# Strassen's seven block products for the second matrix product of an attention and MLP kernel on one core

## The chip, the cores and the metric

One Trainium2 chip, of which the kernel uses one core. The metric is the device time of one execution, in microseconds. Of the kernel before there are three timed runs, with a median of 689.35 us (686.24 to 691.3), and one profiled execution with a span of 687.8 us.

## What is computed

For each of 8 batches there are 8 heads of 512 tokens of 64 numbers, and 32 state rows per head. Tokens read the state and the state reads the tokens, both by softmax attention. The 544 rows of a batch (512 tokens, 32 state rows), with the heads side by side as 512 numbers, then pass through a normalized two-layer MLP with a residual.

```python
scores = scale * np.matmul(x, state.transpose(0, 1, 3, 2))
a = np.exp(scores - scores.max(-1, keepdims=True)); a /= a.sum(-1, keepdims=True) + 1e-09
xread = np.matmul(a, state)
scores2 = scale * np.matmul(state, x.transpose(0, 1, 3, 2))
a2 = ...                                   # the same softmax
sread = np.matmul(a2, x)
x = np.concatenate([xread, sread], axis=2) # then B, S, H*D: 8 x 544 x 512
xn = (x - mu) / np.sqrt(var + 1e-06) * g_ln
out = x + np.maximum(xn @ w_ch1, 0.0) @ w_ch2   # 512 x 2048, 2048 x 512
```

## The kernel before

**Precision.** A number of a large product is held as the sum of two float16 numbers, a high half and a low half. A product is three matmuls, high times high, high times low and low times high (`TERMS`), which add up in PSUM. A high half is made by a ScalarE copy, a low half by an instruction that subtracts the high half from the value.

**Tiles.** The 2048 hidden numbers are 4 units `u` of 512, each of 4 blocks of 128. The 512 tokens of a batch are 4 blocks `c` of 128. `ea` holds the softmax weights of the tokens over the state rows, by two groups `g` of 4 heads.

**Stages of a batch.** `attention` (L225 and on) loads x and state, makes the scores (L320, into a pair of banks called `banks`), transposes them on VectorE (`ts`), subtracts the maximum on GpSimd, takes the exponential on ScalarE, multiplies with the reciprocal sum on GpSimd, and transposes back (`ef`, then `ea`). `ea` is sent by DMA into `ek`, from which L432 makes the residual rows `xr`; bn_stats, `mv`, `rs` and `rf` are its moments. `eb` is the other softmax, for the state rows. `state_products` (L577) multiplies the state with the first weights, into `matrix`: per unit and head group one product L582, one ScalarE copy and one VectorE instruction. The first layer of a batch is then `matrix` times `ea`: `first_products` (L605), L616, 6 matmuls of 512 columns for each of 16 blocks. `hidden` (L595) takes each bank through ScalarE (relu into `strip`, copy to the high half) and VectorE (low half); for batch 0 GpSimd makes the low half. The four units stay in `hid`. `second_products` (L691) has 48 matmuls of 512 columns (L683) per token block in one PSUM bank, one VectorE instruction that scales and adds to `xr`, and a store per two blocks. Batch 0 goes by units (L706), since its weights arrive late. The 256 state rows of all batches come last: `state_hidden` (L648) with L668, matmuls of 256 columns, and the same second product.

**PSUM.** 5 banks `acc`, one pair `banks`, one bank `spread`.

**Order.** Each stage is a stream of instructions. Three strings, `PLAN` (start to batch 1), `BATCH` (2 to 5) and `LAST`, say which piece of which stream is issued next (`issue`, L190). Each engine then works through its own instructions in that order, waiting for those of other engines where they are needed. Nearly all of them pass through one helper and stand at L110 in the profile, and at L166 in the changed kernel.

Of the kernel before, what the change touches and what calls it, by code (L numbers as in the profile page):

```python
# [14 lines left out]
ALU = mybir.AluOpType  # L15
# [12 lines left out]
SW = 2.0**13  # L28
CM = 2.0**-14
SH = 2.0**-12  # L30
SB = 2.0**14
# [74 lines left out]
def do(f, *args, **kw):  # L106

    def now(v):
        return v() if isinstance(v, Later) else v
    return lambda: f(*map(now, args), **{k: now(v) for k, v in kw.items()})  # L110


@with_exitstack
def moe_attention(ctx: ExitStack, tc: tile.TileContext, x, state, g_ln, w1, w2, out):

# [664 lines left out]
```

## Time and profile before

| what | value |
|---|---|
| three runs, median | 689.35 us |
| lowest, highest | 686.24, 691.3 us |
| span of the profiled execution | 687.8 us |
| median less that span | 1.55 us |
| DMA traffic | 69.36 MB, mean 101 GB/s |
| HBM read, written | 28.05 MB, 9.44 MB |

An entry of the page with an engine shows busy time, its share of the span and the count of its instructions. The rows of digits cut the span in 40 equal slices, each digit the busy share in tenths; `PEclk` is the clock that TensorE was granted, 9 for the full one. Rows of groups have line, engine, operation, output and inputs, shapes and count, then busy time and the mean in nanoseconds of one, then the idle time ahead of them and who ended it. A row of the chain has start, length and what ran. A row of the timeline has in brackets how long the engine was idle ahead of it. PE is TensorE, PEld its weight loads, DVE is VectorE, ACT ScalarE, POOL GpSimd. Matmuls overlap, so the spacing of many in a row tells their cost, not the mean of one.

### The profile page before, as it was taken

Reading aid. Unit: us, or ns where it says so; the run is one execution under the profiler, and the core shown is the slowest. Engines: PE = TensorE matmul, PEld = TensorE weight load, DVE = VectorE, ACT = ScalarE, POOL = GpSimd, SP = SyncE. Lnnn points to the kernel's source line nnn. Section 1 sums busy time; section 2 is a strip of 40 time slices with the busy share of each in tenths; the row PEclk is TensorE's granted clock in tenths of the full one; section 3 lists DMA queues with packets and bytes.
Section 4 is the critical chain, followed back from the end, with each engine's and each line's share of the span. In section 5 each row is a group of like instructions: output and inputs, shape, how many; then the busy total and the mean of one; then the engine's idle time right before and its main releaser. Section 6 shows DMA issues by size and latency. Waiting matters only on the chain.

```text
span 687.8 us, 10177 instructions
## 1 busy us (share of the span) xinstructions
PE 646.6 (94%) x4068; PEld 314.3 (46%) x4068; DVE 373.7 (54%) x668; ACT 362.4 (53%) x588; POOL 67.5 (10%) x54
## 2 busy tenths in 40 slices
PE   1667899999999999999999999999999999999997
PEld 0224655544444444444444444444444444447653
DVE  5988999656634447264536544654366834521020
ACT  5387888796422754186327631774168615712120
POOL 0000463400200002000200020001100110100000
PEclk9866999999999999999999999999999999999999
DMA  8989984826061041504151415121590330120011
GB/s 322 286 263 222 245 206 116 164 45 137 31 165 63 1 81 36 159 34 81 31 155 42 81 31 130 66 52 32 141 213 16 68 83 32 61 47 1 1 61 31
DMA packets 98544, 69.36 MB, mean 101 GB/s; under 512 B 72704, under 2 KB 90624, under 8 KB 98048
## 3 DMA queue, kind: packets, MB, share of 16 engines
q1 hardware_dynamic: 96384, 64.77, 36.6%
q0 software_dynamic: 864, 3.15, 2.5%
q10 hardware_dynamic: 1248, 0.79, 0.4%
q8 instruction: 32, 0.52, 0.3%
q14 instruction: 16, 0.13, 0.1%
HBM read 28.05 MB, written 9.44 MB: 55 GB/s over the span
## 4 chain that ended last, share of the span: by engine, by line
PE 84%; DVE 7%; DMA 3%; ACT 3%; issue 1%; SPq 1%; ACTq 0%; DVEq 0%
PE acc L683 48%; PE acc L616 22%; PE acc L582 4%; PE acc L668 3%; PE acc L516 3%; DVE w_t L110 2%; PE banks L396 1%; PE banks L432 1%; PE banks L320 1%; DVE matrix L110 1%; ACT raw L110 1%; PE banks L409 1%; DMA x_f<-in_x_dram 1%; DMA ek<-ek 1%; DVE x L110 1%
## 5 line engine op out<-in xcount | busy, mean ns | idle before, releaser
L683 PE MATMUL acc<-w2h,hid 128*128 128x512 f16 x1632 | 363.4, 379 | 0.0
L683 PEld LDWEIGHTS <-hid 128*128 128x128 f16 x1632 | 157.1, 98 | 192.5 <-issue 9.3
L616 PE MATMUL acc<-ea,matrix 128*128 128x512 f16 (+1 forms) x864 | 175.2, 356 | 0.9 <-DVE matrix L110 0.7
L616 PEld LDWEIGHTS <-matrix 128*128 128x128 f16 x864 | 82.6, 98 | 82.8 <-ACT matrix L110 2.9
L110 DVE TENSOR_TENSOR hid<-strip,hid 128x512 f16<-128x512 f32 x120 | 81.0, 685 | 66.3 <-ACT hid L110 65.7
L110 ACT ACTIVATE strip<-acc,hs 128x512 f32<-128x512 f32 x112 | 75.5, 681 | 53.6 <-PE acc L616 40.4
L110 ACT ACTIVATE hid<-strip 128x512 f16<-128x512 f32 x136 | 82.9, 625 | 15.7 <-PE acc L683 13.6
L110 ACT ACTIVATE matrix<-acc 128x512 f16<-128x512 f32 x64 | 35.7, 599 | 91.6 <-PE acc L582 91.6
L110 DVE SCALAR_TENSOR_TENSOR xr<-acc,of_second,xr 128x512 f32<-128x512 f32 x28 | 20.9, 747 | 88.5 <-PE acc L683 88.4
L110 DVE SCALAR_TENSOR_TENSOR matrix<-acc,matrix 128x512 f16<-128x512 f32 x64 | 42.1, 679 | 11.6 <-ACT matrix L110 11.5
L110 POOL TENSOR_TENSOR ts<-ts,mA 128x1024 f32<-128x1024 f32 (+1 forms) x8 | 14.4, 1802 | 230.6 <-DVE mA L110 230.6
L582 PE MATMUL acc<-w1c,sT 128*32 128x512 f16 x512 | 36.2, 389 | 0.3 <-DMA w1c<-raw 0.3
L110 DVE BATCH_NORM_STATS2 s<-xr 128x6 f32<-128x512 f32 x32 | 21.6, 679 | 16.4 <-ACT xr L110 16.4
L110 POOL TENSOR_TENSOR rs<-rs,mhalf 128x4 f32<-128x4 f32 (+1 forms) x10 | 10.3, 1031 | 192.3 <-DVE rs L110 192.3
L110 POOL TENSOR_TENSOR hid<-strip,hid 128x512 f16<-128x512 f32 x16 | 22.9, 1486 | 45.4 <-ACT hid L110 44.7
L516 PE MATMUL acc<-w_t,gm 128*128 128x512 f32 x32 | 21.0, 823 | 6.3 <-DVE w_t L110 6.3
L110 DVE SCALAR_TENSOR_TENSOR x<-x_f,x_s,x 128x512 f16<-128x512 f32 x32 | 25.7, 833 | 1.9 <-ACT x L110 1.8
L110 ACT ACTIVATE xr<-banks,ux 128x1024 f32<-128x1024 f32 x14 | 15.5, 1109 | 19.7 <-PE banks L432 19.7
L110 ACT ACTIVATE x<-x_f,x_s 128x512 f16<-128x512 f32 x32 | 21.4, 713 | 7.9 <-DVE x_s L110 7.9
L110 ACT ACTIVATE strip<-acc,hr 128x512 f32<-128x512 f32 x8 | 5.4, 684 | 35.6 <-PE acc L668 34.9
L110 DVE TENSOR_REDUCE mB<-banks 128x2 f32<-128x1024 f32 x7 | 8.5, 1217 | 27.9 <-PE banks L320 27.9
L110 ACT ACTIVATE ea<-ef 128x1024 f16<-128x1024 f32 (+1 forms) x9 | 8.6, 960 | 26.6 <-DVE ef L110 26.6
(114 smaller groups left out, 524.1 us busy)
## 6 DMA issues: line engine op xcount, KB each, us to landing
raw<-in_moe_w_ch_dram SPq DMA_DIRECT2D x16, 1024.0 KB, 7.8
out_dram<-xr SPq DMA_DIRECT2D x16, 512.0 KB, 2.7
x_f<-in_x_dram SPq DMA_DIRECT2D x15, 512.0 KB, 5.8
w1c<-raw SPq DMA_DIRECT2D x16, 256.0 KB, 6.2
ek<-ea SPq DMA_DIRECT2D x56, 64.0 KB, 2.0
ek<-ek SPq DMA_DIRECT2D x7, 512.0 KB, 7.7
xr<-part POOLq DMA_DIRECT2D x6, 512.0 KB, 5.9
high<-w1c SPq DMA_DIRECT2D x8, 256.0 KB, 7.2
```

Source lines behind the costliest of these rows:

```text
L110: return lambda: f(*map(now, args), **{k: now(v) for k, v in kw.items()})
L320: nc.tensor.matmul(o[32 * j:32 * j + 32], lhsT=sT[:, g, a, 32 * j:32 * j + 32], rhs=xT[:, s, 4 * g + j].rearrange("p c t -> p (c t)"), sta ...
L396: nc.tensor.matmul(ps_z[:, h // 4, :, h % 4], lhsT=xv[:, c // hc, h, c % hc], rhs=ebT[:, :, h // 4, c, 32 * (h % 4):32 * (h % 4) + 32], st ...
L409: nc.tensor.matmul(pr[:, g], lhsT=z4[:, g, i], rhs=fold, start=i == 0, stop=i == 1, skip_group_check=True)
L432: nc.tensor.matmul(px[:, c, D * h:D * h + D], lhsT=ek[:, h // 4, h % 4, (2 * t + c) * P:(2 * t + c + 1) * P], rhs=sk[:, h], start=True, st ...
L516: nc.tensor.matmul(ps, lhsT=gm[:, k:k + 1].broadcast_to([P, P]), rhs=t4[:, k], start=k == 0, stop=k == 3)
L582: nc.tensor.matmul(ps[32 * j:32 * j + 32], lhsT=sT[:, g, a, 32 * j:32 * j + 32], rhs=w[:, 2 * g + j // 2, j % 2], start=a == 0, stop=a == ...
L616: nc.tensor.matmul(o, lhsT=m[:, g, i, P * q:P * q + P], rhs=ea[:, s, k, g], start=g == 0 and n == 0 and (b > 0 or q % 2 == 0), stop=g == 1 ...
L668: nc.tensor.matmul(ps[:, 256 * f:256 * f + 256].rearrange("p (t n) -> p t n", t=2), lhsT=w[:, k // 2, k % 2, fs] if k < H else wn[:, k - H ...
L683: nc.tensor.matmul(po, lhsT=hid[:, i, q, c * P:(c + 1) * P], rhs=w[:, j, q], start=first and q == 0 and n == 0, stop=last and q == 3 and n ...
```

## The change

For batches 1 to 7 and the state rows the second product is made by Strassen's method: both factors are cut in 2 by 2 blocks, seven products of sums of blocks take the place of eight, and the result is put together by additions. A piece of work is now 256 tokens (a group `g`) and a unit of 512 hidden numbers: 256 × 512 times 512 × 512, in blocks of 128 tokens × 256 and 256 × 256.

- **First product.** `first` (L770) makes 24 matmuls of 256 columns per piece, into a pair of banks named `pair` with one buffer. `state_products` of batches 1 to 7 uses the same pair and reads both halves with one ScalarE and one VectorE instruction of 1024 numbers, where there were two of 512 each. The state rows have `first_of_state` (L779).
- **Sums of the left factor.** One ScalarE relu of 1024 numbers fills `rs`. VectorE makes three sums of 256, GpSimd one. The seven operands `xs`: ScalarE copies the high halves (768 for the three plain blocks, 1024 for the four sums), VectorE makes the low half of the 768 and GpSimd of the 1024. `rs` and `xs` have two buffers each, by turns of the pieces.
- **The seven products.** `strassen_products` (L808): 42 matmuls of 256 columns per piece, in four parts, into four `acc` banks that a group holds over its four units.
- **Putting together.** Per group one ScalarE copy of 512, four VectorE additions from PSUM (256, 512, 256, 512), one GpSimd addition of 256, then two VectorE instructions add to `xr`, and a store.
- **Sums of the right factor.** `sums_of_weights`, once per unit: per half, GpSimd adds the halves (1024) and makes four sums of 256, ScalarE and VectorE make the float16 halves of these, one of which replaces a block of the weights.
- **PSUM** is now 4 banks `acc`, the pair `banks` and the pair `pair`; what used `spread` takes a bank of the others.
- **Scales** `SH`, `SB` and the bound of the second weights change by a factor of two.
- **Order.** One string `PLAN` with entries "stream:index" orders the whole program, written anew for all of it.

The core of the diff:

```diff
+S2 = 2.0**12
-SH = 2.0**-12
-SB = 2.0**14
+SH = 2.0**-13
+SB = 2.0**15
...
 PLAN = (
-    "b3 b0 d0 b1 b4 b2 b5-6 a0 b7-11 b22 b12 b72 b24 b13 b19 b17 d3 b23 d2 b25 b14 b20 b18 d1 d5-6 d4 d7 e1 "
...
+    "1:1 1:3 1:0 1:2 1:4-7 0:0 1:8-12 2:1 2:6 2:0 1:17-18 2:5 2:7 2:3 1:13 1:22-23 2:2 4:1 4:5 1:24 2:4 4:6 1:25 4:7 "
...
-    ps_f = ctx.enter_context(tc.tile_pool(name="ps_f", bufs=5, space=PSUM))
+    ps_f = ctx.enter_context(tc.tile_pool(name="ps_f", bufs=4, space=PSUM))
     ps_a = ctx.enter_context(tc.tile_pool(name="ps_a", bufs=1, space=PSUM))
-    ps_x = ctx.enter_context(tc.tile_pool(name="ps_x", bufs=1, space=PSUM))
+    ps_d = ctx.enter_context(tc.tile_pool(name="ps_d", bufs=1, space=PSUM))
...
+    sums = main.tile([P, 3 * 2048], F32, name="sums")
+    strip = main.tile([P, 3 * 512], F32, name="strip")
...
             for g in range(G):
-                ps = accumulator()
-                yield do(multiply, ps, g, sT, w1c[u])
-                yield do(nc.scalar.activation, m[:, g, 0], ps, AF.Copy, scale=CM)
-                yield do(nc.vector.scalar_tensor_tensor, m[:, g, 1], ps, CM, m[:, g, 0], ALU.mult, ALU.subtract)
+                if b == 0 or g == 0:
+                    two = accumulator() if b == 0 else pair()
+                yield do(multiply, two if b == 0 else two[:, g], g, sT, w1c[u])
+                if b == 0 or g == 1:
+                    ps, v = (two, m[:, g]) if b == 0 else (two, m.rearrange("p g i f -> p i g f"))
+                    v = [v[:, i] for i in range(2)]
+                    yield do(nc.scalar.activation, v[0], ps, AF.Copy, scale=CM)
+                    yield do(nc.vector.scalar_tensor_tensor, v[1], ps, CM, v[0], ALU.mult, ALU.subtract)
...
+    def sums_of_weights(u):
+
+        w = w2h[u].rearrange("p i (k n) e -> p i n k e", n=2)
+        t = unit(u, "w2_sums").rearrange("p (i k e) -> p i k e", i=2, k=2)
+        s = t[:, 1].rearrange("p k (x e) -> p (k x) e", x=2)
+        (b21, b22), (b11, b12) = ([t[:, 0, k, 256 * x:256 * x + 256] for x in range(2)] for k in range(2))
+        for n in range(2):
+            yield do(nc.gpsimd.tensor_tensor, t[:, 0], w[:, 0, n], w[:, 1, n], ALU.add)
+            yield do(nc.gpsimd.tensor_tensor, s[:, 0], b12, b11, ALU.subtract)
+            yield do(nc.gpsimd.tensor_tensor, s[:, 2], s[:, 0], b22, ALU.subtract)
+            yield do(nc.gpsimd.tensor_tensor, s[:, 3], b21, s[:, 2], ALU.add)
+            yield do(nc.gpsimd.tensor_tensor, s[:, 1], b22, b12, ALU.subtract)
+            v = [w[:, i, n, 1, 256:512] for i in range(2)]
+            yield do(nc.scalar.activation, v[0], s[:, 0], AF.Copy)
+            yield do(nc.vector.tensor_tensor, v[1], s[:, 0], v[0], ALU.subtract)
+            v = [sums16[:, u, :, i, n] for i in range(2)]
+            yield do(nc.scalar.activation, v[0], s[:, 1:4], AF.Copy)
+            yield do(nc.vector.tensor_tensor, v[1], s[:, 1:4], v[0], ALU.subtract)
...
+                def strassen_hidden(b=b, g=g, u=u, ps=ps, x=x, r=r, s=s):
+                    if b < B:
+                        yield do(first, ps, g, u, matrix[b][u], ea)
...
+                    yield do(nc.scalar.activation, r.rearrange("p n (k t) e -> p k n (t e)", k=2),
+                             ps.rearrange("p k (n e) -> p k n e", n=2), AF.Relu, scale=(hs if b < B else hr)[:, u:u + 1])
+                    a12, a22, a11, a21 = (r[:, :, k] for k in range(4))
+                    d = r[:, :, 0:3].rearrange("p n k t -> p k n t")
+                    yield do(nc.vector.tensor_tensor, s[:, 0], a11, a21, ALU.subtract)
+                    yield do(nc.gpsimd.tensor_tensor, s[:, 2], a21, a22, ALU.add)
+                    yield do(nc.scalar.activation, x[:, 0:3, :, 0], d, AF.Copy)
+                    yield do(nc.vector.tensor_tensor, s[:, 1], s[:, 0], a22, ALU.subtract)
+                    yield do(nc.vector.tensor_tensor, s[:, 3], a12, s[:, 1], ALU.add)
+                    yield do(nc.vector.tensor_tensor, x[:, 0:3, :, 1], d, x[:, 0:3, :, 0], ALU.subtract)
+                    yield do(nc.scalar.activation, x[:, 3:7, :, 0], s, AF.Copy)
+                    yield do(nc.gpsimd.tensor_tensor, x[:, 3:7, :, 1], s, x[:, 3:7, :, 0], ALU.subtract)
...
+                                nc.tensor.matmul(po[o], lhsT=x[:, o, n, i], rhs=v[j],
+                                                 start=u == 0 and n == 0 and k == 0 and o in (2, 1, 4, 3),
+                                                 stop=u == U - 1 and n == 1 and k == 2, skip_group_check=True)
+                    for ops in ((2, 0, 1), (4,), (3, 5), (6,)):
+                        yield do(lambda po, *a, ops=ops: multiply(ops, [v() for v in po], *a), po, x, w2h[u], sums16[:, u])
...
+                yield do(nc.scalar.activation, c[:, 0:2], two[0], AF.Copy)
+                yield do(nc.vector.tensor_tensor, c[:, 4], bank[1][:, 0:256], c[:, 1], ALU.add)
+                yield do(nc.gpsimd.tensor_tensor, c[:, 1], c[:, 1], c[:, 0], ALU.add)
+                yield do(nc.vector.tensor_tensor, c[:, 2:4], two[2], c[:, 4:5].broadcast_to([P, 2, 256]), ALU.add)
+                yield do(nc.vector.tensor_tensor, c[:, 4], bank[2][:, 0:256], c[:, 3], ALU.add)
+                yield do(nc.vector.tensor_tensor, c[:, 2:4], two[3], c[:, 2:4], ALU.add)
```

Two places show what the new order does. First VectorE in the softmax of one of the middle batches, before:

```order
L110 TENSOR_REDUCE mB_2557<-banks_2540 128x2
L110 SCALAR_TENSOR_TENSOR sk_93<-s_r_2324,x_s_2390,sk_93 64x512
L110 TENSOR_SCALAR mB_2557<-mB_2557,es_2523 128x2
L110 STREAM_TRANSPOSE ts_2588<-banks_2540 128x1024
L110 TENSOR_REDUCE mA_2590<-ts_2588 128x32
L110 SCALAR_TENSOR_TENSOR eb_2597<-eB_2594,eb_2597 128x1024
L110 TENSOR_REDUCE dA_2632<-ts_2588 128x32
L110 TENSOR_TENSOR hid_2525<-strip_2528,hid_2525 128x512
```

The same engine in the group whose first bank is acc_3973, with the change; the `strip` rows put together the group before it (acc_3577 to acc_3580), and matrix_4119 is what the second state product waits for:

```order
L166 TENSOR_TENSOR strip_71<-acc_3578,strip_71 128x512
L166 TENSOR_TENSOR rs_3889<-rs_3889 128x256 x3
L166 SCALAR_TENSOR_TENSOR sk_95<-s_r_3335,x_s_3654,sk_95 64x512
L166 TENSOR_REDUCE dA_4002<-ts_3909 128x32
L166 TENSOR_TENSOR rs_4004<-rs_4004 128x256 x3
L166 TENSOR_TENSOR xs_4010<-rs_3889,xs_4010 128x6x128
...
L166 SCALAR_TENSOR_TENSOR eb_4042<-eB_4028,eb_4042 128x1024
L166 TENSOR_SCALAR rB_4039<-rB_4039,x_i_3652 128x2
L166 TENSOR_TENSOR rs_4071<-rs_4071 128x256
L166 SCALAR_TENSOR_TENSOR matrix_4119<-pair_4096,matrix_4119 128x2x512
```

Where one `hid` row stood between the softmax's rows, the rows of two pieces stand now, and a matrix row behind them all.

Second, GpSimd in the middle batches. Before, a whole batch, from the softmax of one (ts_2588) to that of the next (ts_3278):

```order
L110 TENSOR_TENSOR ts_2588<-ts_2588,mA_2590 128x1024
L110 TENSOR_TENSOR ts_2588<-ts_2588,dA_2632 128x1024
L110 TENSOR_TENSOR rs_2944<-rs_2944,mhalf_84 128x4
L110 TENSOR_TENSOR ts_3278<-ts_3278,mA_3280 128x1024
L110 TENSOR_TENSOR ts_3278<-ts_3278,dA_3322 128x1024
```

With the change, in the softmax of one batch (ts_4869):

```order
L166 TENSOR_TENSOR xs_4953<-rs_4833,xs_4953 128x8x128
L166 TENSOR_TENSOR rs_4838<-rs_4838,mhalf_86 128x4
L166 TENSOR_TENSOR ts_4869<-ts_4869,mA_4901 128x1024
L166 TENSOR_TENSOR rs_4899<-rs_4899 128x256
L166 TENSOR_TENSOR ts_4869<-ts_4869,dA_5066 128x1024
L166 TENSOR_TENSOR xs_5111<-rs_4899,xs_5111 128x8x128
L166 TENSOR_TENSOR rs_4980<-rs_4980 128x256
L166 TENSOR_TENSOR xs_5195<-rs_4980,xs_5195 128x8x128
```

Between and around the two rows of the softmax now stand the additions (rs, 256 numbers) and the low halves (xs, 1024) of the pieces, a pair of rows for each piece of work.

More of the change, by code (lines that the diff above doesn't have):

```diff
@@ L110, in do, with issue @@
     return lambda: f(*map(now, args), **{k: now(v) for k, v in kw.items()})
+def issue(tc, streams, plan):
+    streams = [list(s) for s in streams]
+    with tc.manual_schedule():
+        for item in plan.split() or [f"{k}:0-{len(s)}" for k, s in enumerate(streams)]:
+            k, n = item.split(":")
+            n = [int(v) for v in n.split("-")]
+            for f in streams[int(k)][n[0]:n[-1] + 1]:
+                f()
 @with_exitstack
@@ L172, in odd @@
         return block(8, "residual_1", 1, name)
-    def spare(name):
-        return block(8, "convert", 1, name)
     def accumulator():
@@ new lines, in multiply @@
+                for f in range(2):
+                    for g in range(G):
+                        for n, (i, k) in enumerate(TERMS):
+                            nc.tensor.matmul(o[:, 256 * f:256 * f + 256], lhsT=m[:, g, i, P * (q + f):P * (q + f) + P],
+                                             rhs=ea[:, s, k, g], start=f == 0 and g == 0 and n == 0,
+                                             stop=g == 1 and n == 2, skip_group_check=True)
+            for s in range(2):
+                for q in (0, 2):
+                    ps = accumulator()
+                    yield do(multiply, ps, s, q, matrix[0][u], ea)
+                    yield from hidden(ps, SH, *(h[:, i, q:q + 2, 256 * s:256 * s + 256] for i in range(2)), 2, nc.gpsimd)
@@ new lines, in moe_attention, with high_halves, state_rows @@
+    high, state_rows_T = [None] * U, [None]
+    def high_halves(u):
+        high[u] = quad("high").bitcast(F16).rearrange("p (k f) -> p k f", k=4)
+        for s in range(2):
+            half = slice(64 * s, 64 * s + 64)
+            yield do(nc.sync.dma_start, out=high[u][half], in_=w1c[u][half, :, s])
+    def state_rows():
+        xs = [r[:, 0:1] for r in residual(B, "xs")[1]]
+        results.append(((None, xs),))
+        for t in range(2):
+            yield do(nc.sync.dma_start, out=xs[t][:, 0], in_=sread_rows[P * t:P * t + P, :])
+        xsT = rows("xsT").bitcast(F16)[:, 0:24 * P].rearrange("p (t k n) -> p t k n", t=2, k=12)
+        state_rows_T[0] = xsT
+        mv, rs = yield from moments([xs[t][:, 0] for t in range(2)])
+        xn = rows("xn")
+        for t in range(2):
+            xt = xn[:, DM * t:DM * t + DM]
+            yield do(nc.vector.tensor_scalar, xt, xs[t][:, 0], mv[:, t, 0:1], rs[:, t:t + 1], ALU.subtract, ALU.mult)
+            v = xt.rearrange("p (h d) -> p h d", h=H)
+            pc = halves("pc")[:, 0:12 * P]
+            hi = pc[:, 0:8 * P].rearrange("p (h i d) -> p h i d", h=H, i=2)
+            lo = pc[:, 8 * P:12 * P].rearrange("p (h d) -> p h d", h=H)
+            yield do(nc.scalar.activation, hi, v.unsqueeze(2).broadcast_to([P, H, 2, D]), AF.Copy, scale=SN)
+            yield do(nc.vector.scalar_tensor_tensor, lo, v, SN, hi[:, :, 0], ALU.mult, ALU.subtract)
+            yield do(nc.sync.dma_start_transpose, out=xsT[:, t], in_=pc)
```

246 lines of the change are left out of this document (116 added, 130 removed), and 143 rows, old and new, of tables (BATCH, LAST, PLAN).

## The prediction, made before the changed kernel was run

> **What bounds the kernel now.** First the page: how full each engine is, when, and what the chain that ended last is made of.
>
> ```profile
> span 687.8 us, 10177 instructions
> PE 646.6 (94%) x4068; PEld 314.3 (46%) x4068; DVE 373.7 (54%) x668; ACT 362.4 (53%) x588; POOL 67.5 (10%) x54
> PE   1667899999999999999999999999999999999997
> PEclk9866999999999999999999999999999999999999
> PE 84%; DVE 7%; DMA 3%; ACT 3%; issue 1%; SPq 1%; ACTq 0%; DVEq 0%
> PE acc L683 48%; PE acc L616 22%; PE acc L582 4%; PE acc L668 3%; PE acc L516 3%; DVE w_t L110 2%; PE banks L396 1%; PE banks L432 1%; PE banks L320 1%; DVE matrix L110 1%; ACT raw L110 1%; PE banks L409 1%; DMA x_f<-in_x_dram 1%; DMA ek<-ek 1%; DVE x L110 1%
> ```
>
> TensorE is full from about the sixth slice on, at a full granted clock. The second product (L683) alone is 48% of the chain, the first (L616) 22%. Next the chain in order of time, where rows of back-to-back matmuls give the price of one, and then the steady stretch.
>
> ```profile
> 295.11 1.40 PE acc L616 x6
> ...
> 366.22 1.40 PE acc L616 x6
> ...
> 600.55 20.72 PE acc L683 x96
> ...
> 626.48 5.24 PE acc L668 x48
> ```
>
> ```profile
> 100.00:120.00 20.00, 20.00 (x151) 10.51 (x149) 19.07 (x35) 17.88 (x25) 7.57 (x7) 1.00 0.46 120
> 240.00:320.00 80.00, 80.00 (x486) 36.59 (x484) 42.95 (x78) 43.51 (x76) 4.83 (x3) 1.00 0.31 73
> 320.00:400.00 80.00, 80.00 (x491) 36.53 (x493) 39.44 (x72) 40.37 (x71) 4.84 (x3) 1.00 0.33 77
> 400.00:480.00 80.00, 80.00 (x498) 36.53 (x487) 43.37 (x74) 42.53 (x74) 6.74 (x4) 1.00 0.27 66
> ```
>
> A matmul of 512 columns takes 20.72/96 = 215.8 ns, one of 256 columns 5.24/48 = 109.2 ns. A batch takes 71.1 us (366.22 − 295.11). In the windows the columns after the length are PE, PEld, DVE, ACT and POOL: PE has no gap in 240 us, DVE is busy 41.9 of 80, ACT 42.1, POOL 5.5. So the bound is the number of matmul columns. Only PE counts, as long as the others keep up.
>
> **What PE saves.** 1440 of the 1632 matmuls of L683 go (192 stay for batch 0), 2520 of 256 columns come: 1440 × 215.8 = 310.8 us become 2520 × 109.2 = 275.2, −35.6. The first products of batches 1 to 7, 672 of 512 columns, become 1344 of 256: 145.0 to 146.8, +1.8. The rows of these forms:
>
> ```profile
> L683 PE MATMUL acc<-w2h,hid 128*128 128x512 f16 x1632 | 363.4, 379 | 0.0
> L683 PEld LDWEIGHTS <-hid 128*128 128x128 f16 x1632 | 157.1, 98 | 192.5 <-issue 9.3
> L616 PE MATMUL acc<-ea,matrix 128*128 128x512 f16 x672 | 153.2, 379 | 0.9 <-DVE matrix L110 0.7 <-ACT matrix L110 0.2
> ```
>
> (379 ns is one pipelined matmul's latency; the spacing is 215.8.) A weight load takes 98 ns and each narrow matmul needs its own. The L668 row is such a stream, a load per matmul, and still runs at 109.2, so I take the load as hidden. **Sum for PE: −33.8 us**; a batch would take 71.1 − 4.9 = 66.2 us, a step of one unit and 256 tokens a little over 8.2.
>
> **What the other engines get.** The prices:
>
> ```profile
> L110 DVE TENSOR_TENSOR hid<-strip,hid 128x512 f16<-128x512 f32 x120 | 81.0, 685 | 66.3 <-ACT hid L110 65.7
> L110 DVE TENSOR_TENSOR ts<-ts,dA 128x512 f32<-128x512 f32 x1 | 0.7, 691 | 0.0
> L221 DVE TENSOR_TENSOR fold<-idf 128x64 f32<-128x64 f32 x1 | 0.2, 224 | 0.3 <-POOL idf masks.py:199 0.3
> L110 DVE SCALAR_TENSOR_TENSOR matrix<-acc,matrix 128x512 f16<-128x512 f32 x64 | 42.1, 679 | 11.6 <-ACT matrix L110 11.5
> L110 POOL TENSOR_TENSOR ts<-ts,dA 128x1024 f32<-128x1024 f32 x7 | 13.4, 1911 | 23.4 <-DVE dA L110 22.0 <-DVE of_weights L110 1.4
> L110 POOL TENSOR_TENSOR ts<-ts,dA 128x512 f32<-128x512 f32 x1 | 1.0, 1047 | 2.5 <-DVE mB L110 2.5
> L110 POOL TENSOR_TENSOR hid<-strip,hid 128x512 f16<-128x512 f32 x16 | 22.9, 1486 | 45.4 <-ACT hid L110 44.7 <-DVE raw L110 0.6
> L110 ACT ACTIVATE xr<-banks,ux 128x1024 f32<-128x1024 f32 x14 | 15.5, 1109 | 19.7 <-PE banks L432 19.7
> ```
>
> DVE's 224 ns for 64 elements and 691 for 512 put a 256 one at 0.42, a 768 one at 0.96, a 1024 one at 1.2. POOL's 1047 and 1911 put a 256 one at 0.62; its 1024 low half lies between 1.91 and 2.97 (twice 1486), and I take 2.1. Per step DVE now has three rs adds and the low half of three operands, 2.2 us; POOL one add and the low half of four operands, 2.7; ACT relu and two copies, near 3.0. Per batch DVE gains 8 × 2.2, four matrix low halves at 1.2 and twice the 2.2 of `together`, and loses 16 × 0.685 and 8 × 0.679: 37.3 (41.9 × 71.1/80) becomes about 48 of 66 us. ACT goes from 37.5 to 41, POOL from 4.9 to 28. None alone is full. The question is whether DVE and POOL can be busy at the same time.
>
> ```profile
> 77.95 3.49 POOL L110 TENSOR_TENSOR hid<-strip,hid 128x512 f16<-128x512 f32 x2 [39.74 <-ACT hid L110]
> ```
>
> ```profile
> 78.76 1.66 DVE L110 SCALAR_TENSOR_TENSOR x<-x_f,x_s,x 128x512 f16<-128x512 f32 x1
> ...
> 158.63 0.75 DVE L110 SCALAR_TENSOR_TENSOR x<-x_f,x_s,x 128x512 f16<-128x512 f32 x1
> ...
> 335.88 1.51 DVE L110 SCALAR_TENSOR_TENSOR eb<-eB,eb 128x1024 f16<-128x1024 f32 x1 [1.61 <-ACT eb L110]
> 337.52 1.22 DVE L110 TENSOR_REDUCE dA<-ts 128x32 f32<-128x1024 f32 x1
> ```
>
> The same DVE instruction took 1.66 us where a POOL add ran and 0.75 where none did. Its two tensors lie in SBUF. So do those of most new DVE work: rs and xs 17.8 per batch, the residual 3.0, eb, ea, sk and x about 6.5. With POOL's 28 that is 55 of 66 us if the two exclude each other: enough room on average, little within a step. A DVE tensor_tensor beside POOL is not in the trace; its delay lies between nothing and the rest of the POOL instruction, and I take it as the scalar_tensor_tensor row shows, the nearest kind.
>
> The Trainium skill, "SBUF — State Buffer", section "Who interferes with whom", states that a DVE instruction with two SBUF inputs contends with a GpSimd instruction that reads SBUF, as an exclusive lock for the whole instruction, whoever starts first. The 1.66 against 0.75 agrees; tensor_tensor no row here shows. By the page the delay comes whenever the two meet, which is the second rival below; with no lock it would be the first.
>
> **The heavy groups: +21 us.** Of the 15 groups of 256 tokens, six also carry the next batch's softmax. I walked the one whose second state product goes to pair_4153. That product needs matrix_4119 (the low half on DVE has to have read pair_4096, the pair's only buffer). From the group's first Strassen product PE has 96 narrow matmuls to it (10.5) and one state product (L582: 4% of 687.8 over 512 matmuls, 54 ns each, 16 of them 0.9): 11.4 us. On DVE stand ahead of it, in its order: four adds of `together` (2.2), six rs adds (2.5), sk (0.75), dA (1.2), the xs low half (0.96), eb (1.5), one more rs (0.42) and some ten small ones (2.0): 11.5, and 1.2 of its own, 12.7. That is 1.3 late with no blocking, if each starts when the one before it ends. POOL has 8.3 in the same stretch (two low halves 4.2, the ts multiply 1.9, two adds 1.2, a power 1.0); what does not hide behind DVE's reads of PSUM, its reduction and its small work, up to some 4.5 and waits of a microsecond, comes on top, so 7 at most. What waits is PE's queue: behind that state product stand the rest of the Strassen products. A second heavy group, walked the same way, came to 5. The ends are 0 and 7 per group (in the first, other work of PE hides the 1.3); the walks come to 7 and 5 with blocking and to about 1 without, so the middle, 3.5 × 6 = **21** (0 to 42). Light groups have 8 us a step against DVE's and POOL's 5 together: **+1** (0 to 3).
>
> **The change-over to batch 1: +8 us.** Here the softmax of batch 1 is a chain that PE has to cover:
>
> ```profile
> 176.91 1.17 DVE ts L110
> ...
> 190.87 1.23 DVE ea L110
> ...
> 203.74 0.77 PE banks L432 x16
> ```
>
> From the transposed scores to ea it took 15.2 us, from there to the matmuls on ek 11.6, all under the second product of other units. In the new order PE has after the scores four second products (48 × 215.8 = 10.4) and a state product (0.4) before the first L770, which needs ea: up to 4.3 short. Then 24 matmuls (2.6) and a state product (0.9) before L491, which needs ek: up to 8.0 more. Both together 0 to 12.3; the second gap stands right behind the first and PE's order leaves it nothing else, so I take two thirds, 8. The block sums cost POOL 8 × (1.9 + 4 × 0.62) = 35 us and DVE 11 in that stretch, ahead of the first low halves on POOL's queue; in the window 100 to 120 DVE has 1 us free of 20, POOL 12. Without cover there the first xs would be late, part of the upper end.
>
> **The end: +1.5.** One residual add after the last matmul (of the 0.75 kind) becomes the rest of `together` (an add of 0.69 and the first residual add), and the last low half on POOL has one step to hide in: 1 to 3.
>
> **Sum**, against the profiled 687.8: −33.8 + 21 + 1 + 8 + 1.5 = −2.3, 685.5. The median of the runs is 1.55 above the span, so **687.0**: no change that can be told. 1% is 6.9 us, about what a measurement of this kernel can tell from no change (682.5 to 696.2). The forecast's own range is 680 to 697, which is 2.3 to 5.2 us per heavy group.
>
> **Rivals.** *The cover holds.* ACT and DVE wait little for POOL, the matrices come at most 1.5 late, PE's saving stays: heavy groups 1 each, change-over 5, end and light 3: −33.8 + 14 = −19.8, 669.5 (657 to 682). For it: the steady rows leave DVE half the time free before, x and rs have two buffers, a step of slack. Against it: the pair has one buffer, and the walk is late even without blocking.
>
> *DVE and POOL take turns and become the bound*, in the heavy groups: a low half on DVE stands behind a POOL low half of 2.1 us again and again, 6.5 per group, 39 in all, change-over 10, end and light 4: −33.8 + 53 = +19, 708 (697 to 716), slower. It decides from 5 us per heavy group. For it: the 1.66 us row, and that POOL's share grows sixfold. Against it: transposes, reductions and PSUM reads on DVE are not delayed in the rows beside POOL, and 55 of 66 us leaves 11.
>
> *Narrow matmuls do not run at 109 ns*: were each 5 ns dearer (only 11 ns lie between it and the load's 98), 3864 of them cost 19 us, 707 on the forecast's sum. The L668 row speaks against it.
>
> **Chances.** Forecast 0.37, cover holds 0.36, taking turns 0.22, dear matmuls 0.05. Faster by over 1%: nearly all of the second and a sliver of the first, 0.41; within 1%: 0.28; slower: 0.31. The range goes from 662 (change-over and heavy groups both near nothing) to 713 (all near their upper ends).
>
> **What would show it.** Right: PE's L808 rows at 109 ns back to back; PE idle of 20 to 30 us in six places between 200 and 600 us, released by DVE matrix or xs; a gap of several us before L770 and L491 near 180; DVE rs and xs rows longer than 0.42 and 0.96 where POOL runs. Wrong: PE without gaps in 240 to 480 and a batch in 66 us (the first rival); a period over 72 (the second); L808 rows over 112 ns apart.

## The result, and the profile after

The changed kernel took 741.19 us (median of 4 runs, 740.43 to 744.35) against 690.25 for the kernel before in the same comparison: a ratio of 1.0766, with a 95% interval of 1.0727 to 1.0805. It is 51 us slower; the forecast of 687 and its range to 713 are both missed. The profiled execution has a span of 742.5 us against 687.8 before, 54.7 more. The ratios here and below are of undisturbed executions; a few took far longer, among them the profiled one of e12 (2235 us), whose rows are not used.

The page of the changed kernel, the lines that answer to those shown of before:

```profile
span 742.5 us, 14084 instructions
PE 635.7 (86%) x5818; PEld 491.5 (66%) x5820; DVE 573.0 (77%) x836; ACT 403.0 (54%) x531; POOL 319.4 (43%) x229
PE   2567988674998969988997999898989998999996
PEclk9878989878999989999999999999999999999999
PE 29%; DVE 27%; issue 6%; ACT 5%; DMA 3%; POOL 3%; SPq 3%; DVEq 0%; ACTq 0%; POOLq 0%
```

TensorE is no longer what the chain consists of: 84% became 29%, and VectorE stands beside it with 27%. PE is busy 10.9 us less (635.7 for 646.6), where the count of columns promised 33.8 less, and idle 106.8 us where it was 41.2. So the 54.7 us are −33.8 of work, +22.9 in which the same work ran more slowly, and +65.6 of waiting. Added up by who ended them, PE's waits for VectorE grew from 24.0 to 55.0 us, those for DMA from 3.7 to 21.4 and those for ScalarE from 9.3 to 21.1; GpSimd itself ended 2.4 us of them.

The groups by form, with the count, busy time and mean of one as before:

```profile
L166 POOL TENSOR_TENSOR xs<-rs,xs 128x1024 f16<-128x1024 f32 x60 | 134.1, 2235 | 153.9 <-ACT xs L166 150.1
L166 DVE TENSOR_TENSOR rs<-rs 128x256 f32<-128x256 f32 x180 | 115.4, 645 | 50.0 <-ACT rs L166 47.0
L166 DVE TENSOR_TENSOR xs<-rs,xs 128x768 f16<-128x768 f32 x60 | 79.3, 1322 | 24.2 <-ACT xs L166 17.1
L166 DVE SCALAR_TENSOR_TENSOR matrix<-pair,matrix 128x1024 f16<-128x1024 f32 x28 | 34.0, 1215 | 14.4 <-ACT matrix L166 14.4
L166 POOL TENSOR_TENSOR rs<-rs 128x256 f32<-128x256 f32 x60 | 55.4, 925 | 71.7 <-ACT rs L166 71.7
L166 POOL TENSOR_TENSOR w_sums<-w_sums 128x256 f32<-128x256 f32 x32 | 31.9, 1013 | 9.5 <-DVE w2h L166 5.3
L166 POOL TENSOR_TENSOR w_sums<-w2h 128x1024 f32<-128x1024 f16 x8 | 19.7, 2465 | 5.7 <-PE acc L694 5.5
```

The view of the tile rs has the shortest, the median and the longest of each group:

```profile
L166 DVE TENSOR_TENSOR rs<-rs x180: 360/425/2343, 180.0 to 728.8; 128x256 f32<-128x256 f32 x180
L166 DVE TENSOR_TENSOR xs<-rs,xs x60: 895/952/2877, 179.1 to 729.1; 128x768 f16<-128x768 f32 x60
L166 POOL TENSOR_TENSOR rs<-rs x60: 718/907/1707, 185.3 to 727.3; 128x256 f32<-128x256 f32 x60
```

The medians of VectorE, 425 and 952 ns, are the prices of the forecast (0.42 and 0.96). The means, 645 and 1322, are not: some instances take three to five times as long. The matrix row, one of whose tensors lies in PSUM, has its 1.2 us as priced. Rows of the timeline show an instance each, first VectorE and then GpSimd:

```profile
104.10 0.68 DVE L166 TENSOR_SCALAR raw<-raw 128x1024 uint32<-128x1024 uint32 x1
...
115.38 2.15 DVE L166 TENSOR_SCALAR of_unit<-rf,uoq 128x4 f32<-128x4 f32 x1
...
143.54 3.25 DVE L166 SCALAR_TENSOR_TENSOR sk<-s_r,x_s,sk 64x512 f16<-64x512 f32 x1
```

```profile
115.39 2.12 POOL L166 TENSOR_TENSOR w_sums<-w2h 128x1024 f32<-128x1024 f16 x1
...
142.55 0.72 POOL L166 TENSOR_TENSOR w_sums<-w_sums 128x256 f32<-128x256 f32 x1 [0.45 <-DVE w2h L166]
143.21 0.87 POOL L166 DMA_DIRECT2D xr<-part  x1
143.83 2.41 POOL L166 TENSOR_TENSOR w_sums<-w2h 128x1024 f32<-128x1024 f16 x1
```

`of_unit` is four numbers a partition and ends when GpSimd's addition of 1024 does, at 117.5. `sk`, 0.75 us in the kernel before, started 0.3 us ahead of a GpSimd addition and ended 0.55 us behind it, at 146.8 for 146.2.

The stretch of the start, the kernel before and then the changed one, the windows view with PE, PEld, DVE, ACT, POOL, the clock:

```profile
100.00:200.00 100.00, 100.00 (x626) 47.97 (x623) 67.14 (x123) 69.04 (x108) 21.35 (x19) 1.00 0.46 102
```

```profile
100.00:200.00 100.00, 75.81 (x509) 41.22 (x509) 87.33 (x99) 59.32 (x87) 73.29 (x57) 0.86 0.40 85
140.00:160.00 20.00, 11.81 (x53) 4.06 (x52) 18.75 (x18) 8.37 (x10) 15.97 (x12) 0.66 0.35 67
400.00:500.00 100.00, 96.93 (x1008) 80.46 (x1008) 77.56 (x118) 58.81 (x78) 41.32 (x28) 0.98 0.35 87
```

Here 24 us of waiting arise where there were none, and PE's clock, full before, is 0.86. In the timeline of PE in that stretch:

```profile
171.70 4.33 PE L770 MATMUL pair<-ea,matrix 128*128 128x256 f16 x23 [2.33 <-DVE ea L166]
177.24 1.05 PE L641 MATMUL pair<-w1c,sT 128*32 128x512 f16 x16 [1.20 <-ACT rs L166]
182.06 1.10 PE L491 MATMUL banks<-sk,ek 128*128 128x64 f16 x16 [3.78 <-DMA s_j<-in_state_dram]
```

23 matmuls of 256 columns in 4.33 us are 188 ns each. Where PE has no gap the price is the forecast's, from one start to the next 2.62 us for 24 matmuls, 109 ns:

```profile
731.73 2.78 PE L808 MATMUL acc<-sums,xs 128*128 128x256 f16 x24
734.35 2.13 PE L808 MATMUL acc<-w2h,xs 128*128 128x256 f16 x18
```

The Trainium skill, "TensorE: Matmul & The Clock Gate", section "Part 1: The HAM clock gate (the 'warmup' mystery)", states that TensorE runs at half its clock after an idle window of about 3.4 us until it has been busy for one. Such rows behind a gap, and a clock of 0.66 where PE was 59% busy, agree with a lower clock behind idle time; the length of the window is not shown here, and the gap ahead of the 23 matmuls is 2.33 us.

### The profile page after: what moved, and what is told of

Read it like the earlier page. It is cut to its first block, busy times and chain, and to the rows that moved or that the text cites. A ratio compares the mean times of both kernels' runs of the same rounds, so it can differ in the third digit from the quotient of the medians.

```text
span 742.5 us, 14084 instructions
## 1 busy us (share of the span) xinstructions
PE 635.7 (86%) x5818; PEld 491.5 (66%) x5820; DVE 573.0 (77%) x836; ACT 403.0 (54%) x531; POOL 319.4 (43%) x229
## 3 DMA queue, kind: packets, MB, share of 16 engines
q1 hardware_dynamic: 96384, 64.77, 33.3%
## 4 chain that ended last, share of the span: by engine, by line
PE 29%; DVE 27%; issue 6%; ACT 5%; DMA 3%; POOL 3%; SPq 3%; DVEq 0%; ACTq 0%; POOLq 0%
PE acc L808 15%; PE pair L770 9%; DVE rs L166 7%; DVE xs L166 4%; SPq L166 3%; DVE strip L166 2%; DMA ek<-ek 2%; POOL xs L166 2%; PE pair L641 2%; DVE matrix L166 2%; DVE xr L166 2%; ACT rs L166 1%; DVE x L166 1%; ACT xs L166 1%; DVE mB L166 1%
## 5 line engine op out<-in xcount | busy, mean ns | idle before, releaser
L808 PEld LDWEIGHTS <-xs 128*128 128x128 f16 x2520 | 247.0, 100 | 57.6 <-issue 15.1
L166 POOL TENSOR_TENSOR xs<-rs,xs 128x1024 f16<-128x1024 f32 x60 | 134.1, 2235 | 153.9 <-ACT xs L166 150.1
L808 PE MATMUL acc<-w2h,xs 128*128 128x256 f16 x1440 | 188.4, 278 | 8.9 <-DVE xs L166 6.4
L770 PE MATMUL pair<-ea,matrix 128*128 128x256 f16 x1344 | 160.2, 277 | 8.4 <-ACT rs L166 3.1
L166 ACT ACTIVATE xs<-rs 128x768 f16<-128x768 f32 (+1 forms) x120 | 111.8, 945 | 89.8 <-DVE rs L166 48.1
L166 DVE TENSOR_TENSOR rs<-rs 128x256 f32<-128x256 f32 x180 | 115.4, 645 | 50.0 <-ACT rs L166 47.0
L770 PEld LDWEIGHTS <-matrix 128*128 128x128 f16 x1344 | 132.3, 99 | 28.8 <-issue 8.2
L808 PE MATMUL acc<-sums,xs 128*128 128x256 f16 x1080 | 144.2, 277 | 3.0 <-DVE strip L166 2.8
L166 DVE TENSOR_TENSOR xs<-rs,xs 128x768 f16<-128x768 f32 x60 | 79.3, 1322 | 24.2 <-ACT xs L166 17.1
L694 PE MATMUL acc<-w2h,hid 128*128 128x512 f16 x192 | 48.1, 409 | 4.2 <-DVE w2h L166 3.2
L641 PE MATMUL pair<-w1c,sT 128*32 128x512 f16 x448 | 31.2, 392 | 21.5 <-DVE matrix L166 15.8
L694 PEld LDWEIGHTS <-hid 128*128 128x128 f16 x192 | 19.5, 103 | 31.8 <-issue 13.8
L166 POOL TENSOR_TENSOR w_sums<-w_sums 128x256 f32<-128x256 f32 x32 | 31.9, 1013 | 9.5 <-DVE w2h L166 5.3
```

What stands on the lines that cost most here:

```text
L641: nc.tensor.matmul(ps[32 * j:32 * j + 32], lhsT=sT[:, g, a, 32 * j:32 * j + 32], rhs=w[:, 2 * g + j // 2, j % 2], start=a == 0, stop=a == ...
L694: nc.tensor.matmul(po, lhsT=hid[:, i, q, c * P:(c + 1) * P], rhs=w[:, j, q], start=first and q == 0 and n == 0, stop=last and q == 3 and n ...
L770: nc.tensor.matmul(ps[:, q // 2, 256 * (q % 2):256 * (q % 2) + 256], lhsT=m[:, h, i, P * q:P * q + P], rhs=ea[:, 0, k, h, 256 * g:256 * g ...
L808: nc.tensor.matmul(po[o], lhsT=x[:, o, n, i], rhs=v[j], start=u == 0 and n == 0 and k == 0 and o in (2, 1, 4, 3), stop=u == U - 1 and n == ...
```

## The experiments

The theory, formed on these rows: GpSimd's reads of SBUF and VectorE's instructions take **turns**, VectorE's queue falls behind, PE waits for it, and behind the waits its clock is low. Rivals: the new **order** with its long queues and one `pair` makes the waits, whoever reads; the dense narrow matmuls lower the **clock** by themselves. The ratio is to the kernel before on the same chip.

| experiment | us | ratio to before, 95% interval |
|---|---|---|
| the change | 741.2 | 1.0766 (1.0727 to 1.0805) |
| e1: GpSimd only writes in the pieces | 707.9 | 1.0256 (1.0210 to 1.0301) |
| e2: its work of the pieces on VectorE | 762.9 | 1.1058 (1.0991 to 1.1125) |
| e3: sums and low halves on 8 columns | 701.1 | 1.0170 (1.0141 to 1.0199) |
| e4: before, with narrow matmuls | 694.0 | 1.0071 (1.0044 to 1.0097) |
| e5: GpSimd only writes in the weight sums | 727.9 | 1.0547 (1.0497 to 1.0597) |
| e6: e1 and e5 together | 693.6 | 1.0065 (1.0041 to 1.0089) |
| e7: weight sums on PE | 764.3 | 1.1081 (1.1036 to 1.1126) |
| e8: pieces read from PSUM | 964.8 | 1.3992 (1.3945 to 1.4039) |
| e10: e1, weight sums left out | 701.7 | 1.0179 (1.0117 to 1.0241) |
| e11: before, with GpSimd's work | 757.3 | 1.0970 (1.0922 to 1.1017) |
| e12: e11, reading another tile | 692.5 | 1.0063 (1.0037 to 1.0088) |
| e13: e3, weight sums left out | 692.0 | 1.0027 (0.9996 to 1.0057) |

**e1, GpSimd writes only.**

```diff
-yield do(nc.gpsimd.tensor_tensor, s[:, 2], a21, a22, ALU.add)
+yield do(nc.gpsimd.memset, s[:, 2], 1.0)
-yield do(nc.gpsimd.tensor_tensor, x[:, 3:7, :, 1], s, x[:, 3:7, :, 0], ALU.subtract)
+yield do(write_twice, x[:, 3:7, :, 1])     # two memsets of the place
```

> GpSimd's two instructions of a piece (the sum of 256 and the low half of 1024) only write constants, the low half's place twice over, so the products are made of other numbers; instructions, dependencies and order are those of the changed kernel, but GpSimd reads no SBUF in the pieces. Theory of turns (GpSimd's reads of SBUF and VectorE's instructions with two SBUF tensors exclude each other): VectorE's rs mean falls from 645 ns to 425, its xs mean from 1322 to about 950, VectorE's busy time from 573 us to under 500, the time from 741 us to 690 to 710, since the block sums of the weights still read. Theory of the order (long queues and one pair buffer make the waits, whoever reads): 730 us or more, PE idle near 107 us as before.

707.9 us, 33.3 less. In its profile the groups of the pieces:

```profile
L801 POOL MEMSET xs<- 128x1024 f16 x60 | 57.1, 951 | 3.4
L166 DVE TENSOR_TENSOR rs<-rs 128x256 f32<-128x256 f32 x180 | 83.4, 469 | 62.0 <-ACT rs L166 59.0
L166 DVE TENSOR_TENSOR xs<-rs,xs 128x768 f16<-128x768 f32 x60 | 58.9, 982 | 33.0 <-ACT xs L166 21.6 <-PE acc L811 4.7 <-POOL rs L166 3.3
```

GpSimd is about as long at the low half (twice 0.95 us for 2.2), in the same place of every queue, and VectorE's instructions are back near their medians. Its busy time fell from 573.0 to 496.4 us. That GpSimd's reading held these rows up, and not the length of its work, is shown by this. That a GpSimd instruction which only writes does not contend with a VectorE instruction with two SBUF inputs is what the page "SBUF — State Buffer" of the Trainium skill states in "Who interferes with whom", and these rows agree.

The 33 us are not the reading alone, though, and the dependencies are not quite those of the change, as the expectation has it. A write waits neither for the relu nor for ScalarE's copy: GpSimd waited 150.1 us for the copy ahead of the low halves, and here 145.1 us for PE to free their place. And the write in place of the sum takes 0.31 us for 0.925. Since GpSimd ended only 2.4 us of PE's waits in the change, little of the gain should come that way directly; how much does is not shown. The same holds of e5 and e6.

**e2, all of it on VectorE.** The three instructions take `nc.vector` in place of `nc.gpsimd`.

> The sum, the low half of the four sums and the addition of the putting together go from GpSimd to VectorE; nothing is left out. Theory of turns: VectorE takes 60 x (0.42 + 1.2) = 98 us more of its own and loses the blocked 80 us or so, so that its busy time stays near 590 us and the low halves come earlier, 1.2 us long in place of 2.2: 715 to 740 us. Theory of the order: VectorE is the longest queue already, so it is slower than the changed kernel, 755 us or more.

762.9 us: slower than the change, as the rival had it, and 23 us above what the theory of turns allowed. VectorE's busy time was 586.0, as the theory of turns had it: the turns cost as much of VectorE's time as the work itself would. But the work then stands in one queue, and PE waited more for `xs` (14.9 us for 6.4). To move GpSimd's work to VectorE is no way out.

**e3, small sums**, and **e4, narrow matmuls in the kernel before.**

```diff
-yield do(nc.vector.tensor_tensor, s[:, 0], a11, a21, ALU.subtract)
+yield do(nc.vector.tensor_tensor, s[:, 0, :, 0:8], a11[:, :, 0:8], a21[:, :, 0:8], ALU.subtract)
...
-nc.tensor.matmul(po[o], lhsT=x[:, o, n, i], rhs=v[j],
+nc.tensor.matmul(po[o], lhsT=x[:, o, n, 0], rhs=v[j],
```

> All sums and low halves of the pieces are made on 8 of 128 columns only, and the products take high halves in place of low ones; the number of instructions, PE's work and the order stay. What remains is PE's own work, the start with the block sums of the weights, the softmax and ScalarE. Both theories: 665 to 690 us, the rest above 655 being the stretch from 100 to 200 us. Theory of the clock (a dense stream of narrow matmuls, each with its weight load, lowers the granted clock by itself): the clock stays near 0.95 in stretches where PE has no gap, and the time over 695 us.

```diff
-nc.tensor.matmul(po, lhsT=hid[:, i, q, c * P:(c + 1) * P], rhs=w[:, j, q],
+for e in (0, 256):
+    nc.tensor.matmul(po[:, e:e + 256], lhsT=hid[:, i, q, c * P:(c + 1) * P], rhs=w[:, j, q, e:e + 256],
```

> The kernel before, with each second product's matmul of 512 columns as two of 256 with the same weights loaded twice: 3264 matmuls at 109.2 ns in place of 1632 at 215.8, 4 us more. Without an effect on the clock: 690 to 697 us, clock 0.979. Theory of the clock: a clock below 0.97 after the start, and 700 us or more.

e4 took 694.0 us with a mean clock of 0.980, 5 us over the kernel before, against 4 worked out: twice as many weight loads lower neither rate nor clock. The theory of the clock falls. e3 missed what was expected of it: 701.1 us with almost all of the pieces' sums gone, 11 us above the upper end of the expected range. So there was a second loss, which the elementwise work of the pieces does not explain.

**e5 and e6, the weight sums.** All five GpSimd instructions of a half write constants, twice each place; e6 is this and e1.

```diff
-yield do(nc.gpsimd.tensor_tensor, s[:, 0], b12, b11, ALU.subtract)
+yield do(twice, s[:, 0])                   # and so the four others
```

> GpSimd's five instructions of each half of the weight sums only write constants, each place twice, so the weight sums are other numbers; the rest is the changed kernel. Theory of turns: in 100 to 180 us VectorE is no longer stretched by GpSimd's reads (its w2h rows of 1024 go from 1.9 us to 1.3, small instructions from 1 to 2 us to 0.2), the first Strassen product starts 15 to 25 us earlier than 183 us, and the time is 715 to 728 us. Theory of the serial start (batch 1 has to wait for the sums and for the buffers that they share, whoever reads): first Strassen product within 6 us of 183, 735 us or more.

> Both: neither in the weight sums nor in the pieces does GpSimd read SBUF; the numbers are others in both. Theory of turns: the two gains add up, 741 less 33 (measured with the pieces alone) less 15 to 25: 682 to 693 us, and PE idle near the 41 us of the kernel before. Theory of the serial start: 702 us or more.

e5 gained 13.3 us and moved the first Strassen product from 183.0 to 166.8 us; e6 gained 47.6, where the two alone add up to 46.6. With all of the added VectorE work still done, but no reads by GpSimd in the pieces and the weight sums, the kernel is at 693.6, 48 us faster than the change. It is still not faster than before.

**e7 and e8, two ways to do without the turns, nothing left out.** e7 makes the weight sums with matmuls by plus and minus the identity. e8 takes VectorE's first operands from PSUM:

```diff
-yield do(nc.vector.tensor_tensor, s[:, 0], a11, a21, ALU.subtract)
+yield do(nc.vector.scalar_tensor_tensor, s[:, 0], v, 0.0, a21, ALU.max, ALU.subtract)   # v: the block in the pair
```

> The weight sums are made on PE, 22 matmuls of 256 columns per half with plus or minus the identity (176 in all, 19 us at 109 ns), into the pair, from which ScalarE and VectorE take the halves; GpSimd has no part in them, nothing is left out; the pieces are as in the changed kernel. Theory of turns: GpSimd's 52 us in the start are gone, PE's 19 us fall in its idle 24, VectorE is not stretched: 710 to 728 us. Theory of the serial start: the sums still stand between batch 0 and batch 1, 735 us or more.

> From batch 2 on VectorE takes the plain blocks of a piece straight from the pair in PSUM (relu in the same instruction), so that each of its six instructions of a piece has at most one SBUF tensor; the unit's scale sits in the matrix; a pair is then free only after VectorE's last low half, 3.5 us or more after its matmuls in place of 1.3, and the next first product is issued behind it; GpSimd is as in the changed kernel, nothing is left out. Theory of turns: VectorE's instructions keep 0.42 us beside GpSimd and the time falls to 705 to 728 us. Theory of the pair (its one buffer is what PE waits for): slower than the changed kernel, 745 us or more.

Both are slower than the change. In e8 the instructions from PSUM, beside GpSimd's unchanged work, and in the same kernel those of the pieces that still read two tensors in SBUF:

```profile
L191 DVE SCALAR_TENSOR_TENSOR rs<-pair,rs 128x256 f32<-128x256 f32 x144 | 60.6, 421 | 179.6 <-ACT rs L191 177.0
L834 DVE SCALAR_TENSOR_TENSOR xs<-pair,xs 128x256 f16<-128x256 f32 x144 | 51.6, 414 | 27.6 <-ACT xs L191 27.6
L191 DVE TENSOR_TENSOR rs<-rs 128x256 f32<-128x256 f32 x36 | 21.2, 597 | 15.5 <-ACT rs L191 14.8
```

421 and 414 ns against 597: the turns are gone as forecast. But PE waits for the pair, in its list of waits (us in total, times, longest), in an order that was made anew for this run:

```profile
PE pair L799 <- DVE xs L834: 82.6, 25, 8.0
PE pair L669 <- DVE matrix L191: 30.3, 12, 3.0
PE pair L669 <- DVE xs L834: 23.9, 8, 5.8
```

The rival of the one buffer decides there. In e7 the added matmuls filled no gap: PE is busy 19 us longer than in the change (654.9 for 635.7) and idle as long (108.5 for 106.8), and it waits 9.5 us of that for the pair that a sum still holds. Three of the four units' sums had to be issued later, where the pair is free, so e7 does not tell what the sums on PE would cost in a plan made for them. That stays untried.

**e10 and e13, what is left.** The weight sums are left out on all engines (two constants per half), with e1's pieces in e10 and e3's in e13.

> As with no GpSimd reads in the pieces, and the weight sums are left out altogether on GpSimd, ScalarE and VectorE (two short constants per half stand in their place), so the products take other numbers; PE's work and the order stay. Theory that what is left of the loss in the start is the time of the sums themselves: first Strassen product by 158 us or earlier (170 with the sums unread, 183 in the changed kernel), 670 to 683 us. Theory that it is the new order of batch 1 (its softmax, ek and the buffers that it shares with batch 0 have too little of PE's work over them): first Strassen product within 6 us of 170, 687 to 695 us.

> The sums and low halves of the pieces on 8 of 128 columns, the products with high halves only, and the weight sums left out (constants): hardly any of the added VectorE and GpSimd work is left, PE's work and the order stay. Theory that the rest of the loss (693 us with no GpSimd reads, against 654 by PE's work alone) is the order of the start, where the softmax of batch 1 and its ek have too little over them, and the slower clock behind gaps: 682 to 692 us, first product of Strassen's near 170 us, PE idle 60 us or more. Theory that it is VectorE's added load even without turns: 660 to 675 us.

e10 came out at 701.7, above both expectations and 8 us above e6, which does more, with the first Strassen product at 175 us: the time of the sums is not what is left. e13 has hardly any added work on VectorE and GpSimd, and still 692.0. In its timeline of PE:

```profile
160.45 0.40 PE L762 MATMUL pair<-ea,matrix 128*128 128x256 f16 x1 [3.55 <-DVE matrix L166]
161.68 5.07 PE L762 MATMUL pair<-ea,matrix 128*128 128x256 f16 x23 [0.84 <-DVE ea L166]
167.95 1.05 PE L641 MATMUL pair<-w1c,sT 128*32 128x512 f16 x16 [1.20 <-ACT rs L166]
173.28 1.13 PE L491 MATMUL banks<-sk,ek 128*128 128x64 f16 x16 [4.28 <-DMA s_j<-in_state_dram]
```

```profile
100.00:200.00 100.00, 83.98 (x602) 49.99 (x602) 59.56 (x102) 58.84 (x81) 28.90 (x37) 0.88 0.42 91
400.00:500.00 100.00, 100.00 (x1009) 83.57 (x1007) 62.05 (x144) 62.14 (x81) 18.98 (x32) 1.00 0.34 78
```

From 400 to 500 PE has no gap: the plan holds there, with 33 us per group of 168 products. From 100 to 200 it is idle 16 us and its clock is 0.88, though VectorE is busy only 60: it waits for the weights, for the matrix, for ea and for ek in the softmax of batch 1. That fits the order, as expected of e13, but part of it is made by the run itself. Just ahead of the waits for the matrix and ea stand on VectorE and GpSimd:

```profile
148.53 8.42 DVE L166 TENSOR_SCALAR hs<-uoq,r 128x4 f32<-128x4 f32 x1
```

```profile
150.08 6.84 POOL L728 MEMSET sums<- 128x768 f16 x10
```

`hs` is four numbers a partition, 0.23 us in the kernel before. It began during a GpSimd multiplication and ends with the last of the ten constants behind it, which GpSimd writes in place of the sums, and the transpose, the matrix and ea stand behind it. In e10 it took 9.56 us and in e6 1.88, so this is the likely reason of e10's 6.7 us of waiting for a matrix, a wait that e6 has not. So e10 and e13 are probably too slow as measures of what is left; by how much is not shown. Nor does e13 separate the order from the new division of PSUM (four `acc` for five, one `pair`): no run has another order or other banks.

**e11 and e12, GpSimd's work in the kernel before.**

```diff
+nc.gpsimd.tensor_tensor(scratch[:, 0:256], f, f2, ALU.add)            # f, f2: of the strip; e12: of hid's high half
+nc.gpsimd.tensor_tensor(scratch, scratch, scratch, ALU.subtract)      # 384 columns, twice
+nc.gpsimd.tensor_tensor(scratch[:, 0:256], f, f2, ALU.add)
```

> The kernel before, to which GpSimd's work of the pieces is added on a scratch tile: 60 times two sums of 256 and two differences of 384, 2.9 us in all each time, the sums reading the strip that VectorE and ScalarE read; the outputs are the reference's. Theory of turns: VectorE's low halves (hid, 685 ns) and the residual additions grow by a third or more, VectorE's busy time from 374 to 420 to 460 us, and the time stays within 1.5% of the kernel before, because VectorE has half its time free there: the turns cost only where VectorE is full. Theory that GpSimd's reads cost time by themselves: 20 us or more slower. Theory that a tensor_tensor is not held up: mean of hid under 720 ns.

> As the run before with GpSimd's work added to the kernel before, but the sums read the high half in hid, whose buffer lives for a whole unit, in place of the strip, which the relu wants back at once (in that run the relu waited 86 us for GpSimd). Theory of turns, with cost only where VectorE is full: hid rows stay near 880 ns, VectorE busy near 415 us, the time within 1.5% of the kernel before, 688 to 700 us. Theory that GpSimd's reads cost time by themselves: over 715 us here too.

e11 was 69 us slower, and missed for a reason of its own:

```profile
L608 DVE TENSOR_TENSOR hid<-strip,hid 128x512 f16<-128x512 f32 x120 | 104.8, 883 | 91.7 <-ACT hid L110 91.0
L110 ACT ACTIVATE strip<-acc,hs 128x512 f32<-128x512 f32 x112 | 75.7, 681 | 120.8 <-POOL scratch L614 86.3 <-PE acc L628 13.7 <-DVE hid L608 12.4
```

VectorE's tensor_tensor grew from 685 to 883 ns, but the relu also waited 86.3 us for the strip, which GpSimd now read last. e12, the same work without that wait, took 692.5, 0.6% over the kernel before. Where VectorE has half its time free, GpSimd's added work costs next to nothing; that the hid rows were near 880 ns there too, as expected, is not shown.

## Why the prediction was wrong, point by point

**PE's own saving** held in count and rate: 109 ns where the clock is full, and −33.8 us of work. That its clock would stay full was not said, and was assumed, a term put at nothing: 22.9 us went there, behind the gaps. The link is read from the traces (full clock without gaps in e4, 0.66 to 0.91 in windows with gaps); no run varied the gaps alone.

**The prices** held as medians. The step that failed is the size of the turns, in "heavy groups: +21" and "light groups: +1". They were counted as an effect on one wait in six groups. All 60 pieces bear it: rs and xs alone cost VectorE 180 × 0.22 + 60 × 0.37 = 62 us. It meets the small instructions too, which the forecast had as "ten small ones (2.0)" and as work behind which GpSimd hides: the 117 TENSOR_SCALARs of at most 32 columns took 45.3 us in all, 25.8 before. The trace of before already had one, of two numbers, held until a GpSimd multiplication ended:

```profile
544.34 1.54 DVE L110 TENSOR_SCALAR rB<-sumB 128x2 f32<-128x2 f32 x1
```

```profile
543.95 1.91 POOL L110 TENSOR_TENSOR ts<-ts,mA 128x1024 f32<-128x1024 f32 x1 [28.36 <-DVE mA L110]
```

Measured by e1, with what its writes change besides: 33 us in place of 22. The sign that was named for it came: PE was idle 33 us from 200 to 600 us (1 before; 20 to 30 had been said for six places), 15.8 us of its waits over the whole span being for the matrix that VectorE makes.

**The change-over: +8** is the step that failed most. It was worked out as two gaps in PE's order with a cover that was taken from durations of before. In the change PE is idle 24 us from 100 to 200 us, where it had no gap before, and its clock is 0.86 there. The weight sums were priced at GpSimd's undisturbed 35 us and mentioned only as part of the upper end; they took 51.6 (19.7 and 31.9), and their reads cost 13.3 (e5). With no sums and few turns, e13 is still 36 us above what PE's saving would give (692.0 against 690.25 − 33.8 = 656.4), as 24 us more idle time, most of it in 100 to 300 us, and 12 of slower work over its whole span. What of this is the order, what the division of PSUM and what the turns that e13 still has, stays open.

**The sum.** −33.8; +48 from the change to e6, for GpSimd's reads (33 in the pieces, 13 in the sums, 1 for both); +2 from e6 to e13, for VectorE's added work; +36 from e13 to PE's saving alone, for the start and the clock behind its gaps. These steps are taken between the same runs, so they have to add up to the 51 that was measured, and that they do is no check. The 2 is too small and the 36 too large by whatever `hs` cost e13, which no run shows.

**The rivals.** "Taking turns" named the right mechanism and the right side, at 0.22, and its sign came, a period over 72: seven batches from the first L770 (169.1 us) to the first L779 (682.9) took 73.4 us each. But its 708 had 39 us in six groups and 10 for the change-over. "The cover holds" is what e13 shows between 400 and 500 us. "Dear matmuls" is refuted by e4. The average that spoke against the turns, 55 of 66 us, was no protection: VectorE was busy 77% of the span and GpSimd 43%, and PE waited for VectorE all the same.

## What to carry to other kernels

If added work puts GpSimd reads of SBUF beside VectorE work on SBUF tensors, count the two as one queue in every stretch, the small instructions included, and not only where a wait is seen. Price a new order by its worst stretch, here the start, where PE was idle 24 us of 100, and add the slower clock behind each gap. A run in which the suspect instruction writes in place of reading, at the same length and in the same place, tells a turn from a long queue, if the write is also made to wait for what the read waited for; and look in its trace for small instructions that the writes hold up.

## What the runs showed of the hardware that was not expected

A VectorE TENSOR_SCALAR on four numbers a partition took 2.15 us beside a GpSimd addition of 2.12, and one on 1024, which reads one tensor, took 1.23 for 0.68 beside two additions of 256: not only instructions with two large tensors in SBUF are held up. GpSimd is slowed in turn: its 256 addition, 0.62 us worked out, took 0.72 at the shortest and 0.925 in the mean.

Writes held up TENSOR_SCALARs, and did not hold up the low halves. In e6, where GpSimd writes the place of a low half twice:

```profile
479.90 0.86 DVE L166 TENSOR_SCALAR rf<-rs,x_i 128x4 f32<-128x4 f32 x1
480.70 0.96 DVE L166 TENSOR_TENSOR xs<-rs,xs 128x768 f16<-128x768 f32 x1
```

```profile
479.79 0.95 POOL L804 MEMSET xs<- 128x1024 f16 x1 [1.44 <-PE acc L815]
480.80 0.95 POOL L805 MEMSET xs<- 128x1024 f16 x1
```

`rf`, four numbers, 0.22 us at the shortest, ends with the first write; the low half beside the second has its undisturbed 0.96. The 8.42 us of `hs` in e13 are the longest case.
